# Attention queries against the keys' sums: 64-column weights in two halves of the array, in place of 128-column weights

## The chip, the cores and the metric

The kernel runs on one core of one Trainium2 chip. The metric is the device time of one execution in microseconds (us), as the median of several executions; beside it stands one execution that was recorded by the hardware profiler.

## What is computed

Three layers follow each other: linear attention, a mixture of experts with two experts per token, and a two-layer network with a squared ReLU. The change is in the first, which is computed for 4 batches, 8 heads, 576 tokens and a head dimension of 64:

```python
def phi(x):
    proj = np.einsum('bhsd,df->bhsf', x, w_phi)          # 128 features
    proj = proj - np.max(np.abs(proj), axis=-1, keepdims=True)
    return np.concatenate([np.exp(proj), np.exp(-proj)], axis=-1)   # 256 features
q_p, k_p = (phi(q), phi(k))
kv = np.einsum('bhsf,bhsd->bhfd', k_p, v)
z = np.sum(k_p, axis=2)
num = np.einsum('bhsf,bhfd->bhsd', q_p, kv)
den = np.einsum('bhsf,bhf->bhs', q_p, z)[..., None] + 1e-06
return (num / den).astype(np.float32)
```

`num` and `den` together are the queries' product with the keys' sums: for each token and head, 256 query features times a matrix that holds `kv` (64 columns), the 16 columns of the two gates already multiplied in, and `z` (1 column), 81 columns in all. That product is what the change touches.

## The kernel before

All of the attention is in fp32. Of the 576 tokens of a batch, 512 are handled as four rows of 128 tokens (`R = 4`), and the last 64 of each batch (the tail) are put together with those of the neighbouring batch.

The attention is a loop over slots `n` from 0 to 37, written out by hand as a software pipeline. A batch has nine units `u` (`i = 0` is the tails, `i = 1` to `8` the rest), and in a slot several units are at work, each at another stage. TensorE (PE) gets its instructions in this order in a slot:

- `kq_a(n)`: transposes of the next K and Q tiles (L388, L393, L399, L403) into the PSUM tile `Tk`, which ScalarE (ACT) copies to `kth` (L407).
- `k_b(n)`: K times `w_phi` into `kpair` (weights on 64 partitions, `64*128` in the profile). VectorE (DVE) takes the maximum `kmx` (L426) and subtracts it (`kd`, L428), ACT makes the two exponentials `kp` (L440, L441).
- `q_b(n - 2)`: Q times `w_phi` into `qpair`; ACT copies it to `ps` (L506), GpSimd (POOL) makes the maximum `qmx` (L508), two slots later DVE subtracts it (L513), and ACT makes the exponentials `qp` (L525, L526).
- `k_c(n - 1)`: the keys' sums into the PSUM tile `KV`, with 64-column weights (`128*64`, the values `vt` and `vtt`) and, in every second unit, 32-column weights (`128*32`, sums of the features, `zs` and `kpt` by `ones`).
- `k_d(n - 2)`, in every second unit: the keys' sums times a small matrix into `Tk` (L98 `gmat`, then `sel`), which ACT copies to `kvc` (L495). `Tk` is the one tile that the next slot's `kq_a` writes too.
- `q_d(n - 5)`: the product of the queries' features `qp` with `kvc`, into one of the PSUM tiles `N0` and `N1`, in turn. 32 such blocks are in the program. DVE divides the result by `den` with four instructions (`norm`, L532 to L544).
- In some slots then `q_tail` (the same product for the tails) and `r_3b` (the routing's ranks of tokens, from `rt_mask`).

The routing (functions `r_0` to `r_6`) runs on DVE in between, a group of four or five rows of tokens at a time, and POOL scatters finished rows to the experts' input `xg_d`. Weights of the first experts are loaded and split (L144, L145) in the same slots. After the loop, the last three units are done among the routing of the last groups, and the first expert's matmuls begin (L98 `M`).

`mm` (L98) issues one matmul; its fp32 matmuls here show as two weight loads and two streams each. The weights of `q_d` are 128 tokens' features, on 128 partitions and 128 columns (`128*128` in the profile), and `kvc`'s 81 columns are streamed past them. `q_tail` has its product in the form with 64-column weights already: two batches' tails lie in partitions 0 to 63 and 64 to 127 of the output.

Of the kernel before, what the change touches and what calls it, by code (L numbers as in the profile page):

```python
# [32 lines left out]
def kernel(  # L33
# [48 lines left out]
    def bank(tag, shape):  # L82
        if tag not in PAIRS:
            return psum.tile(shape, FT, tag=tag, name=tag)
        if pair is None:
            return pbank.tile(shape, FT, tag=tag, name=tag)
        i, half = PAIRS[tag]
        if i and mbank is not None:
            return mbank.tile(shape, FT, tag=tag, name=tag)
        names = "abc"[:len(shape) - 1]  # L90
        n = 1
        for x in shape[1:]:
            n *= x
        return pair[i][:, half, :n].rearrange(
            f"p ({' '.join(names)}) -> p {' '.join(names)}", **dict(zip(names, shape[1:])))

    def mm(o, l, r, start, stop):
        nc.tensor.matmul(o, l, r, start=start, stop=stop, skip_group_check=True)  # L98
# [157 lines left out]
    with ExitStack() as actx:  # L256
# [114 lines left out]
        KH, KP, KPT, KVB, KVZ, KVC, ZS, KE = {}, {}, {}, {}, {}, {}, {}, []  # L371
# [41 lines left out]
        def q_col(j, n):  # L413

            return j % 2 * 256 + j // 2 * n
# [114 lines left out]
        def norm(t, xo, lo):  # L530
            den = ap_.tile([128, 4], FT, name="den", tag="den", bufs=2)
            nc.vector.tensor_scalar(den, t[:, :, 80], 1e-6, None, op0=OP.add)  # L532
            yield
            rec = ap_.tile([128, 4], FT, name="rec", tag="rec", bufs=2)
            nc.vector.reciprocal(rec, den)
            yield
            if len(xo.shape) == 4:
                t = t.rearrange("p (h r) c -> p h r c", h=2)
                rec = rec.rearrange("p (h r) -> p h r", h=2)[:, :, :, None]
            else:  # L540
                rec = rec[:, :, None]
            nc.vector.tensor_mul(xo, t[..., :64], rec.to_broadcast(list(xo.shape)))
            yield
            nc.vector.tensor_mul(lo, t[..., 64:80], rec.to_broadcast(list(lo.shape)))  # L544
            yield

        def q_d(u):
            b, i = divmod(u, 9)
            if i == 0:
                return  # L550
            if i == 1:
                X[b] = ap_.tile([128, R, DM], FT, name="x", tag="x", bufs=2)
                LL[b] = ap_.tile([128, R + 1, 16, H], FT, name="ll", tag="ll", bufs=2)
            t = bank(f"N{(i - 1) % 2}", [128, R, 81])
            qp = QP.pop(u)
            half, hp = LQ[i - 1]
            for j in range(R):
                h = i - 1 if b < B - 1 else 2 * hp + j // 2
                for a in range(2):
                    mm(t[:, j], qp[:, a, q_col(j, 128):q_col(j, 128) + 128],  # L560
                       KVC[b][:, a, h // 2, (h % 2) * 81:(h % 2) * 81 + 81], j == 0 and a == 0, a == 1)
            if b < B - 1:
                ND.append(norm(t, X[b][:, :, h * 64:h * 64 + 64], LL[b][:, :R, :, h]))
            else:
                r = slice(2 * half, 2 * half + 2)
                ND.append(norm(t, X[b][:, r, hp * 128:hp * 128 + 128].rearrange("p r (h d) -> p h r d", h=2),
                               LL[b][:, r, :, 2 * hp:2 * hp + 2].rearrange("p r e h -> p h r e")))
# [253 lines left out]
        for n in range(NU + 2):  # L821
# [3 lines left out]
            b, i = divmod(n, 9)  # L825
# [43 lines left out]
            if 0 <= n - QC < NU:  # L869
                q_d(n - QC)  # L870
# [18 lines left out]
        norms(r_0(g - 1), n=1)  # L889
        q_c1(u)  # L890
        q_d(u - 2)
        r_1(g - 1)
        q_c2(u)
        q_tail(B - 1, 1, "M1")
        norms(r_2(g - 1))
        x_t(0, 0)
        x_t(0, 1)
        q_d(u - 1)
        norms(r_top(g - 1, 0))
        hold()  # L900
# [319 lines left out]
    with tc.If(most > CAP):  # L1220
        with ExitStack() as sctx:
# [27 lines left out]
            with tc.For_i(0, NT, 128) as row:  # L1249
# [8 lines left out]
                for e in range(E):  # L1258
# [4 lines left out]
                    for f in range(F // 128):  # L1263
                        t = bank(f"M{f % 2}", [128, 128])
# [3 lines left out]
                    t = bank("P", [128, DM])  # L1268
# [5 lines left out]
                for n in range(F2 // GF):  # L1274
# [4 lines left out]
                    for f in range(GF // 128):  # L1279
                        t = bank(f"M{f % 2}", [128, 128])  # L1280
# [43 lines left out]
```

## Time and profile before

| | |
|---|---|
| time, median of 3 | 1079.59 us (1079.37 to 1081.08) |
| time of the profiled execution | 1081.6 us |
| its span, first to last instruction | 1079.8 us |
| PE busy | 1057.1 us |
| DVE busy | 599.4 us |
| ACT busy | 473.9 us |
| POOL busy | 396.5 us |
| attention: end of the last `q_d` block, from the span's start | about 209.5 us |

PE is TensorE's streaming of matmuls, PEld its weight loads, which run beside the streams. Busy time of PE is modelled at the end of each matmul (an instruction's end reaches beyond the start of the next), so what a block costs is read from the start of the block to the start of the next one.

### The profile page before, as it was taken

To read this page: it belongs to the slowest core of one execution; us is meant where nothing else is said; L and a number is where in the kernel's file an instruction comes from. 1 tells how busy PE (TensorE), PEld (TensorE's weight loads), DVE (VectorE), ACT (ScalarE), POOL (GpSimd) and SP (SyncE) were. 2 spreads that over 40 slices of the span, in tenths; PEclk is the share of its full clock that TensorE was granted. 3 is DMA by queue.
4 is the path that set the end of the run, shared out by engine and by line. 5 is a ranking of instruction groups with operands and counts; after the bars stand their busy time and mean duration, and the time that the engine had idled before them with its cause. 6 is when DMAs were issued, how large, how long until landed. Compare 5 with 4: busy or idle time off the path is not lost.

```text
span 1079.8 us, 17573 instructions
## 1 busy us (share of the span) xinstructions
PE 1057.1 (98%) x6620; PEld 894.2 (83%) x6620; DVE 599.4 (56%) x1192; ACT 473.9 (44%) x967; POOL 396.5 (37%) x374
## 2 busy tenths in 40 slices
PE   7999999999999999999999999999999999999997
PEld 4777777888988888888888888888988888888885
DVE  5677788832677777686877753432443332333222
ACT  4777677424445353535354545432332222222221
POOL 3343637546645555554555464650010010000000
PEclk9999999999999999999999999999999999999999
DMA  5977524256465656565556554430120111001001
GB/s 138 269 200 220 178 80 152 98 197 207 158 198 181 210 166 205 182 204 183 187 185 198 183 164 127 126 88 1 59 69 11 39 39 40 20 0 39 1 1 41
DMA packets 104044, 136.20 MB, mean 126 GB/s; under 512 B 17554, under 2 KB 58642, under 8 KB 103954
## 3 DMA queue, kind: packets, MB, share of 16 engines
q1 hardware_dynamic: 98194, 116.14, 34.7%
q0 software_dynamic: 5760, 18.88, 5.5%
q8 instruction: 54, 0.88, 0.4%
q14 instruction: 36, 0.29, 0.1%
HBM read 92.45 MB, written 42.54 MB: 125 GB/s over the span
## 4 chain that ended last, share of the span: by engine, by line
PE 94%; DVE 3%; ACT 1%; DMA 0%; issue 0%; SPq 0%; ACTq 0%
PE M L98 38%; PE N L98 18%; PE KV L98 14%; PE Tq L98 8%; PE P L98 8%; PE kpair L98 2%; PE qpair L98 1%; PE Tk L98 1%; PE M L200 1%; PE Tk L393 1%; PE Tk L403 1%; PE Tk L1049 1%; PE Tk L200 1%; DMA kt<-in_k_dram 0%; DVE kd L428 0%; DVE kmx L426 0%
## 5 line engine op out<-in xcount | busy, mean ns | idle before, releaser
L1070 DVE TENSOR_TENSOR r<-M,r 128x512 f32<-128x512 f32 (+1 forms) x80 | 51.1, 638 | 248.3 <-ACT h2h L1069 248.3
L1066 ACT ACTIVATE r<-M 128x512 f32<-128x512 f32 (+1 forms) x80 | 44.5, 556 | 250.9 <-PE M L98 250.9
L229 ACT ACTIVATE hh<-M 128x304 fp32r<-128x304 f32 (+2 forms) x128 | 49.0, 422 | 210.7 <-PE M L98 210.7
L226 DVE SCALAR_TENSOR_TENSOR hl<-M,hh 128x304 fp32r<-128x304 f32 (+2 forms) x128 | 56.1, 470 | 109.4 <-ACT hh L229 109.3
L508 POOL PARTITION_ALL_REDUCE qmx<-ps x36 | 70.0, 1944 | 92.5 <-ACT ps L506 79.6
L1031 POOL DMA_INDIRECT ya<-y_d,yrows x18 | 18.0, 998 | 189.3 <-PE Tk L1049 113.6
L98 PE MATMUL N<-kvc,qp 128*128 128x81 f32 x512 | 63.7, 278 | 1.7 <-DVE runs L698 1.1
L98 PEld LDWEIGHTS N<-kvc,qp 128*128 128x128 f32 x512 | 59.6, 192 | 5.6 <-issue 4.6
L1071 DVE TENSOR_TENSOR h2l<-r,h2h 128x512 fp32r<-128x512 f32 (+1 forms) x80 | 57.7, 722 | 7.0
L1069 ACT ACTIVATE h2h<-r 128x512 fp32r<-128x512 f32 (+1 forms) x80 | 47.1, 589 | 2.6
L98 PE MATMUL M<-x,w30h 128*128 128x512 f32 (+1 forms) x160 | 46.1, 372 | 0.0
L98 PE MATMUL M<-x,w10h 128*128 128x512 f32 (+1 forms) x160 | 45.9, 371 | 0.0
L98 PE MATMUL M<-x,w20h 128*128 128x512 f32 (+1 forms) x160 | 45.8, 371 | 0.0
L98 PE MATMUL M<-x,w00h 128*128 128x512 f32 (+1 forms) x160 | 45.5, 369 | 0.0
L145 POOL TENSOR_TENSOR w30l<-wstage,w30h 128x512 fp32r<-128x512 f32 x20 | 27.7, 1386 | 46.3 <-ACT w30h L144 46.2
L145 POOL TENSOR_TENSOR w20l<-wstage,w20h 128x512 fp32r<-128x512 f32 x20 | 27.9, 1394 | 43.0 <-ACT w20h L144 29.4
L426 DVE TENSOR_REDUCE kmx<-kpair 128x4 f32<-128x512 f32 x36 | 24.8, 689 | 25.5 <-PE kpair L98 25.3
L767 POOL DMA_INDIRECT xg_d<-x,slots x32 | 32.4, 1014 | 12.2 <-issue 5.1
L145 POOL TENSOR_TENSOR w10l<-wstage,w10h 128x512 fp32r<-128x512 f32 x16 | 22.7, 1417 | 38.2 <-ACT w10h L144 35.2
L1001 POOL TENSOR_TENSOR wd<-wd 128x256 f32<-128x256 f32 x32 | 23.6, 737 | 35.0 <-DVE wd L997 35.0
L1001 POOL TENSOR_TENSOR wx<-wx 128x256 f32<-128x256 f32 x32 | 23.6, 738 | 34.3 <-DVE wx L997 34.0
L98 PE MATMUL KV<-kp,vt 128*64 128x256 f32 x256 | 35.6, 400 | 0.0
(432 smaller groups left out, 3271.7 us busy)
## 6 DMA issues: line engine op xcount, KB each, us to landing
wstage<-in_moe_w_dram SPq DMA_DIRECT2D x128, 256.0 KB, 3.8
xg_d<-zero SPq DMA_DIRECT2D x8, 1216.0 KB, 7.5
y_d<-y SPq DMA_DIRECT2D x32, 256.0 KB, 2.3
wide<-in_moe_w_in_dram SPq DMA_DIRECT2D x32, 256.0 KB, 3.4
wide<-in_moe_w_out_dram SPq DMA_DIRECT2D x32, 256.0 KB, 2.9
xg<-xg_d SPq DMA_DIRECT2D x7, 1024.0 KB, 6.3
kt<-in_k_dram SPq DMA_DIRECT2D x16, 256.0 KB, 4.3
vt<-in_v_dram SPq DMA_DIRECT2D x16, 256.0 KB, 4.0
```

Source lines behind the costliest of these rows:

```text
L98: nc.tensor.matmul(o, l, r, start=start, stop=stop, skip_group_check=True)
L145: (nc.gpsimd if n >= 2 else nc.vector).tensor_sub(lo[:, c], src, hi[:, c].bitcast(FT))
L226: nc.vector.scalar_tensor_tensor(hl[:, c0:c1], o, 0.0, hh[:, c0:c1].bitcast(FT), op0=OP.max, op1=OP.subtract)
L229: nc.scalar.activation(hh[:, c[1]:c[2]], c[0], AF.Relu)
L426: nc.vector.tensor_reduce(mx, t, axis=AX.X, op=OP.max, apply_absolute_value=True)
L508: nc.gpsimd.partition_all_reduce(mx, ps, 128, bass.bass_isa.ReduceOp.absmax)
L767: st = nc.gpsimd.indirect_dma_start(out=xg_d, out_offset=bass.IndirectOffsetOnAxis(ap=slots[:, T0[g] + i, c:c + 1], axis=0), in_=src, in_o ...
L1001: nc.gpsimd.tensor_mul(part, part, exp)
L1066: nc.scalar.activation(r[:, :n], t[:, :n], AF.Relu)
L1069: nc.scalar.activation(hh[:, :n], r[:, :n], AF.Square)
L1070: nc.vector.tensor_mul(r[:, :n], t[:, :n], r[:, :n])
L1071: nc.vector.tensor_sub(hl[:, :n], r[:, :n], hh[:, :n].bitcast(FT))
```

## The change

In `q_d`, each product of a row of 128 tokens is issued as two products of 64 tokens. The first has its output in partitions 0 to 63, the second in 64 to 127, and both stream the same 81 columns of `kvc`. The number of `mm` calls in a block goes from 8 to 16; the values computed are the same.

```diff
             for j in range(R):
                 h = i - 1 if b < B - 1 else 2 * hp + j // 2
                 for a in range(2):
-                    mm(t[:, j], qp[:, a, q_col(j, 128):q_col(j, 128) + 128],
-                       KVC[b][:, a, h // 2, (h % 2) * 81:(h % 2) * 81 + 81], j == 0 and a == 0, a == 1)
+                    for s in range(2):
+                        c = q_col(j, 128) + s * 64
+                        mm(t[s * 64:s * 64 + 64, j], qp[:, a, c:c + 64],
+                           KVC[b][:, a, h // 2, (h % 2) * 81:(h % 2) * 81 + 81], j == 0 and a == 0, a == 1)
```

## Rows read from the trace of the kernel before

**Rows 1.** The page's first part: busy us, share of the span, instructions.

```profile
PE 1057.1 (98%) x6620; PEld 894.2 (83%) x6620; DVE 599.4 (56%) x1192; ACT 473.9 (44%) x967; POOL 396.5 (37%) x374
```

**Rows 2.** The chain that ended last, 30 to 215 us, by line.

```profile
by line: PE N L98 27.6%; PE KV L98 22.9%; PE kpair L98 9.7%; PE qpair L98 6.7%; PE Tk L98 5.5%; PE Tk L393 3.5%; PE Tk L403 3.3%; DVE kd L428 1.9%; DVE kmx L426 1.8%; DVE ps L513 1.3%; DVE x L542 1.2%; PE M L98 1.0%; DVE rt_u L654 0.8%; ACT
```

**Rows 3.** Tile N: duration ns min/median/max, first and last start us, forms.

```profile
L98 PEld LDWEIGHTS N<-kvc,qp x512: 186/192/192, 34.4 to 209.3; 128*128 128x128 f32 x171
L98 PE MATMUL N<-kvc,qp x512: 236/275/338, 34.4 to 209.4; 128*128 128x81 f32 x171
L98 PEld LDWEIGHTS N<-kvc,qpt x64: 132/136/137, 110.3 to 118.1; 128*64 128x64 f32 x64
L98 PE MATMUL N<-kvc,qpt x64: 231/233/284, 110.3 to 118.1; 128*64 128x81 f32 x64
```

**Rows 4.** Timeline of PE, 163 to 173 us: start us, us, instructions in order.

```profile
163.77 0.62 PE L98 MATMUL KV<-zs,ones 128*32 128x128 f32 x16
164.32 2.01 PE L98 MATMUL N<-kvc,qp 128*128 128x81 f32 x16
166.17 0.38 PE L393 MATMUL Tk<-ident,kt 128*128 128x128 f32 x2
...
169.88 0.28 PE L98 MATMUL Tk<-sel,kvz 128*128 128x4 f32 x2
170.02 1.99 PE L98 MATMUL N<-kvc,qp 128*128 128x81 f32 x16
171.85 0.38 PE L393 MATMUL Tk<-ident,kt 128*128 128x128 f32 x2
172.06 0.38 PE L403 MATMUL Tk<-ident,qt 128*128 128x128 f32 x2
```

**Rows 5.** Timeline of PE, 110 to 119 us, with a block of q_tail.

```profile
115.09 2.01 PE L98 MATMUL N<-kvc,qp 128*128 128x81 f32 x16
117.03 1.34 PE L98 MATMUL N<-kvc,qpt 128*64 128x81 f32 x32
118.30 0.44 PE L393 MATMUL Tk<-ident,kt 128*128 128x128 f32 x2
118.58 0.38 PE L403 MATMUL Tk<-ident,qt 128*128 128x128 f32 x2
```

**Rows 6.** Timeline of PEld, the weight loads of that q_tail block.

```profile
117.03 1.18 PEld L98 LDWEIGHTS N<-kvc,qpt 128*64 128x64 f32 x32
```

**Rows 7.** Timeline of PE, 196 to 212 us: a change of form behind sel.

```profile
197.60 0.28 PE L98 MATMUL Tk<-sel,kvz 128*128 128x4 f32 x2
197.82 0.70 PE L98 MATMUL qpair<-kth,wf 64*128 64x256 f32 x4
```

**Rows 8.** PE's waits, 20 to 212 us: us in total, times, longest.

```profile
PE Tk L393 <- ACT kvc L495: 1.4, 4, 0.5
PE N L98 <- DVE runs L698: 1.1, 1, 1.1
PE N L98 <- DVE rt_mask L667: 1.0, 2, 0.5
```

**Rows 9.** Timeline of PE: two places where it waited, in brackets for what.

```profile
103.55 0.18 PE L98 MATMUL N<-rt_mask,before 128*128 128x32 bf16 x1 [0.47 <-DVE rt_mask L667]
...
133.64 0.44 PE L393 MATMUL Tk<-ident,kt 128*128 128x128 f32 x2 [0.29 <-ACT kvc L495]
```

**Rows 10.** Timeline of all engines, 143.5 to 145.2 us: kvc, and the next transposes.

```profile
143.31 0.44 ACT L495 ACTIVATE kvc<-Tk 128x324 f32<-128x324 f32 x1
...
144.96 0.38 PE L393 MATMUL Tk<-ident,kt 128*128 128x128 f32 x2
```

**Rows 11.** DVE's longest wait, 20 to 212 us: us in total, times, longest.

```profile
DVE kmx L426 <- PE kpair L98: 17.9, 17, 2.2
```

**Rows 12.** Busy us by stretch: PE, PEld, DVE, ACT, POOL; granted clock, DMA share, GB/s.

```profile
140.00:180.00 40.00, 39.13 (x408) 30.16 (x406) 35.37 (x99) 30.12 (x58) 23.37 (x24) 1.00 0.43 129
...
197.00:212.00 15.00, 14.49 (x174) 13.75 (x174) 13.41 (x71) 6.78 (x15) 7.52 (x13) 1.00 0.20 73
```

## The prediction

> **What bounds the kernel now.** I read the page's first part, then the chain that ended last, then the stretch in which the changed code runs. PE is busy for 98% of the span and DVE, the next, for 56% [rows 1], but that is an average over three layers, and the change touches only the attention. There the reader is to see two things. First, the chain from 30 to 215 us runs mostly along PE, and its largest share, 27.6%, is the line of the blocks that are changed [rows 2]. Of those 185 us that is 51. Second, PE hardly waits: over 20 to 212 us the three longest entries of its waits come to 3.5 us [rows 8], while DVE waits for PE's `kpair` 17 times, 17.9 us in all [rows 11]. So in this stretch PE's own stream of instructions sets the pace, and what is taken out of it is time gained, as long as the others can follow.
>
> How long a block of `q_d` holds PE is read from its start to the start of what comes next: 1.85 us from 164.32 to 166.17, behind `zs`, and 1.83 us from 170.02 to 171.85, behind `sel` [rows 4]. Sixteen weight loads with their streams take it, 0.116 us each. A load of 128 columns is recorded with 192 ns, one of 64 columns with 136 ns [rows 3]. The streams are the same 81 columns in both forms, so the larger load is what stretches the block.
>
> **What the change costs and gives.** It moves nothing to another engine and issues no DMA. It replaces 16 load-and-stream pairs in each of 32 blocks by 32 of the smaller form. That form stands in this trace: `q_tail` has the same 64-column weights on 128 partitions and the same 81 columns, two halves of the output in turn [rows 3]. A block of it has exactly 32 pairs, and takes from 117.03 to 118.30, 1.27 us [rows 5]. I take that as the price of a new block. It carries one difference that no row shows: in `q_tail` the two halves stream the `kvc` of two batches, in the new `q_d` both stream the same one. I see no reason for a price; the bound from above is the second rival.
>
> The form costs changes of mode at its ends, which the block of before did not have. Behind it, the transposes' first load is no longer issued ahead: from the K transposes to the Q transposes it takes 0.28 us behind `q_tail` [rows 5] and 0.21 behind `q_d` [rows 4]: 0.07 us more. In front of it, behind `sel`, `q_d` starts 0.14 us after `sel` did in the same form [rows 4], while a `qpair` of another form starts 0.22 after it [rows 7]. So 0.08 us is added there. Behind `zs` there was a change of form before and there is one now, so I add nothing.
>
> The Trainium skill, "TensorEngine Tiling (Array Packing)", section Tiling Modes, says that a change of tiling mode, other than a change of tile, drains TensorE; that speaks against this change. The rows above agree that it costs something, and give its size, 0.08 in front and 0.07 behind; without these the sum below would be 14.9 us and not 12.6.
>
> Now the 32 blocks by what stands around them, from the slots' order:
>
> - Nine behind `k_c`, followed by transposes of full tiles or by `k_d`: 1.85 - 1.27 - 0.07 = 0.51 each, 4.6 us. (Two of them stand behind sums with 64-column weights, where a change of mode even goes away; I leave that out.)
> - Fourteen behind `sel`: 1.83 - 1.27 - 0.07 - 0.08 = 0.41 each. Three of them are followed by a wait of PE for something that the block does not delay: twice for `rt_mask`, as at 103.55, and once for `kvc`, at 133.64 [rows 9]. There the block ends earlier and PE waits longer, and the gain is lost. Eleven remain, 4.5 us.
> - Three behind `zs` and followed by the K tails' transposes, which are in a third form. Here the block held PE as long as the one ahead of `q_tail`, which also ends in a change of form, 1.94 us [rows 5]; 1.94 - 1.27 = 0.67 each, 2.0 us.
> - Two followed by `q_tail`: now block and follower have the same form, and a change goes away at the seam, which I put at 0.1 us (the two above cost 0.07 and 0.08). 1.94 - 1.17 = 0.77 each, 1.5 us.
> - Four at the loop's end, 198 to 209.5 us. Here DVE is busy for 13.41 of 15 us [rows 12], with the last units' norms and the routing, one instruction behind the other. I count nothing for them. If PE did set the pace there, 0.6 each, 2.4 us, would be added.
>
> That is 12.6 us. What hides the rest of the work is the slack of the other engines. The nearest is `kvc`: ACT ends it at 143.75, and the transposes that write the same PSUM tile start at 144.96, 1.2 us later [rows 10]; the block between them becomes 0.4 us shorter, so 0.8 is left. Behind those transposes PE has all of the next slot queued, so a `kvc` that came later than that would cost its whole delay. DVE is the one that may fall short. From 140 to 180 us it is busy for 35.37 of 40 us [rows 12]. Six of the paying blocks lie there, 2.8 us of gain, and DVE's idle time of 4.6 us covers that only where it falls in the right slots. Around the routing groups it will not fully. I take 0.5 us off for this, one block's gain: 12.1 us.
>
> The profiled execution took 1081.6 us, with a span of 1079.8; its time would be 1069.5. The median of the runs is 1079.59, 0.2% below the profiled one; the same 12.1 us off give **1067.5 us**, and that is my forecast. What follows the attention starts 12.1 us earlier and is the same: PE stays the bound there [rows 1].
>
> **Bounds.** From above: the three lost blocks (1.2 us) and the four at the end (2.4) pay as well, the 0.5 is not lost, and the changes of mode cost half (1.1 less): 17.3 us, 1062.3. From below: DVE stops the gain wherever it is busy for over 85% of the time, in 140 to 180 us, which loses 2.8, and as much again is lost in the 50 us ahead of it, where other routing groups and the weights' splitting run on DVE: 12.1 - 2.8 - 2.8 = 6.5, 1073.1.
>
> **Rivals.**
>
> 1. *DVE becomes the pace of the attention.* For it: 88% busy in 140 to 180 us [rows 12], and waits of PE for DVE that exist already [rows 8]. Against: DVE waits for `kpair` in 17 of some 36 slots, 1.05 us in the mean [rows 11], twice what a block saves. With about half the gain lost: 6.5 us, 1073.1. It decides where DVE's work no longer fits into the shorter slot: the one from 164.32 to 170.02 [rows 4] has 5.7 us, DVE's 88% of it are 5.0, and it becomes 5.2.
>
> 2. *The two halves do not run side by side.* They stream the same `kvc` columns from the same partitions, and if PE took them one after the other, 32 streams would go at the pace of one. In `q_tail` 16 pairs of streams take some 1.12 of the 1.27 us, 0.07 a pair; alone in a row, each of the 32 would take that, 2.24 us, and with the 0.15 that are left of the 1.27 for the changes of mode 2.4: 0.55 more than before, times 28 blocks, 15 us slower, 1095. It decides where a pair takes more than about 0.1 us instead of 0.07: 1.85 less 0.15 and 0.07, over 16. Against it: the 32 loads of `q_tail`, 136 ns each, are done in 1.18 us [rows 3, 6], so loads and streams of the two halves overlap there. The Trainium skill, "TensorE: Matmul & The Clock Gate", Part 3, section The mechanism, says that loads overlap with running matmuls only when the row group differs; both halves here use all rows, so by that rule the loads would add to the streams and this rival would come out. The loads of that block disagree with it for this form [rows 6].
>
> 3. *The pairs run at twice the pace of before.* If two 64-column halves cost no more than half of two full ones, a block would be 1.85 / 2 = 0.93 us; 28 blocks save 0.92 each, 26 us, 1054. The Trainium skill's tiling page named above gives up to 2 times for a small dimension of at most 64 (section Overview). Against it, the rows of `q_tail` in the very form: 1.27 us [rows 5].
>
> 4. *The block is hidden anyway*, and PE waits as much more as it works less. It would need another engine to end last in most slots; the chain says otherwise [rows 2]. Within 2.2 us of 1079.6.
>
> **How the numbers follow.** My forecast (a gain of 8 to 17.3 us) 0.80; DVE sets the pace (2.2 to 8 us) 0.11; side by side fails (slower) 0.04; twice the pace 0.02; hidden 0.03. What a measurement of this kernel can tell from no change is about 0.2%, 2.2 us. The range reaches from the upper bound of the gain to the DVE case, 1062.3 to 1073.1, which leaves out about 2 in 10. Faster: 0.80 + 0.11 + 0.02 = 0.93; within 0.2%: 0.03; slower: 0.04.
>
> **What would show it.** In the changed kernel's profile: the blocks of `N<-kvc,qp` with 1024 loads and streams of the form `128*64`, loads of about 136 ns, and 1.27 us from a block's start to the next start; behind `sel` a start 0.2 us after it; the K transposes behind a block 0.27 us apart from the Q transposes. The last `q_d` block should end near 197.4 us. If DVE is the pace, DVE's waits for `kpair` will be nearly gone and PE's waits for `rt_mask`, `runs`, `zs` or `kvc` will have grown from 3.5 us to 7 or more. If the halves do not run side by side, the block will be 2 us or longer. I would be wrong if a block is not near 1.27 us, or if the time between 212 us and the end changes by more than 1 us.

## The result and the profile after

The changed kernel takes 1068.3 us (median of four runs, 1067.45 to 1069.16), the kernel before, beside it on the same chip, 1080.03 (1079.37 to 1081.08). The ratio is 0.9891, 95% interval 0.9873 to 0.9908: 11.7 us faster. Forecast were 1067.5, with a range of 1062.3 to 1073.1.

The profiled execution after took 1067.83 us, its span 1066.0. That is 13.8 us shorter than the profiled one of before, 2 us more than the medians say. The third layer's first matmul (`M<-x,w00h`) starts at 654.9 us after and at 667.4 before, 12.5 earlier, and 0.65 of that is start-up: the first `q_d` block starts at 33.77 instead of 34.42. In the profiles of all kernels of this study what follows that matmul took between 410.9 and 412.4 us, whichever form the blocks had. So for readings within a microsecond a milestone in the stage is the better measure, not the span of one execution. I take the stretch from the first `q_d` block to the rank matmul of the last routing group (`qpair<-rt_mask,before`, at 211.65 before and 199.17 after): 177.2 us before and 165.4 after, 11.8 shorter. Below it is "the stretch", each time of one execution.

The page's first part of the kernel after (answers to [rows 1]: 512 more matmuls and as many loads, 18 us less of PE), and the chain from 30 to 200 us by line ([rows 2]):

```profile
PE 1038.9 (97%) x7132; PEld 874.8 (82%) x7132; DVE 595.0 (56%) x1192; ACT 471.1 (44%) x967; POOL 396.7 (37%) x374
...
by line: PE KV L98 18.1%; PE N L98 12.7%; PE kpair L98 8.4%; PE qpair L98 5.5%; DVE kd L428 4.9%; PE Tk L98 4.6%; DVE kmx L426 4.5%; PE Tk L393 4.3%; DVE ps L513 3.5%; PE Tk L403 3.2%; ACT kp L440 2.2%; DVE x L542 2.2%; DVE zs L450 2.1%; AC
```

The line of the blocks was the first of the chain with 27.6% and has 12.7% now. DVE's `kmx`, `kd` and `ps` had 5.0% together [rows 2] and have 12.9%: PE still leads, and DVE is much closer behind it.

The forms of tile `N` after (duration ns min, median, max; first and last start; forms), to be read against [rows 3]:

```profile
L98 PEld LDWEIGHTS N<-kvc,qp x1024: 132/137/138, 33.8 to 195.1; 128*64 128x64 f32 x171
L98 PE MATMUL N<-kvc,qp x1024: 230/233/285, 33.8 to 195.2; 128*64 128x81 f32 x171
```

PE's timeline after, around a block behind `zs`, one behind `sel`, and one ahead of `q_tail` (answers to [rows 4, 5]):

```profile
107.85 1.34 PE L98 MATMUL N<-kvc,qp 128*64 128x81 f32 x32
109.02 1.29 PE L98 MATMUL N<-kvc,qpt 128*64 128x81 f32 x32
110.24 0.44 PE L393 MATMUL Tk<-ident,kt 128*128 128x128 f32 x2
...
154.22 0.62 PE L98 MATMUL KV<-zs,ones 128*32 128x128 f32 x16
154.77 1.34 PE L98 MATMUL N<-kvc,qp 128*64 128x81 f32 x32
156.04 0.44 PE L393 MATMUL Tk<-ident,kt 128*128 128x128 f32 x2
156.32 0.38 PE L403 MATMUL Tk<-ident,qt 128*128 128x128 f32 x2
...
159.81 0.28 PE L98 MATMUL Tk<-sel,kvz 128*128 128x4 f32 x2
160.02 1.34 PE L98 MATMUL N<-kvc,qp 128*64 128x81 f32 x32
161.29 0.44 PE L393 MATMUL Tk<-ident,kt 128*128 128x128 f32 x2
161.56 0.38 PE L403 MATMUL Tk<-ident,qt 128*128 128x128 f32 x2
```

A block takes 1.27 us (154.77 to 156.04, 160.02 to 161.29), and 1.17 ahead of `q_tail`. From `sel` to the Q transposes it was 2.18 us [rows 4] and is 1.75.

What PE waited for after, from 20 to 200 us, and DVE's wait for `kpair` (us in total, times, longest; answers to [rows 8, 11]):

```profile
PE Tk L393 <- ACT kvc L495: 4.0, 6, 1.1
PE N L98 <- DVE rt_mask L669: 1.9, 2, 1.0
PE qpair L98 <- DVE rt_mask L669: 1.3, 1, 1.3
PE N L98 <- DVE runs L700: 1.1, 1, 1.1
PE M L98 <- DVE xtl L102: 0.8, 1, 0.8
PE M L200 <- DVE ll L544: 0.7, 1, 0.7
PE N L98 <- ACT kvc L495: 0.5, 1, 0.5
...
DVE kmx L426 <- PE kpair L98: 9.8, 11, 1.7
```

PE's waits come to 10.3 us. The same list of before comes to 4.5, of which the three entries in [rows 8] are 3.5. DVE's wait for `kpair` fell from 17.9 to 9.8 us. So PE's saving went to two places, the kernel's time and longer waits of PE; DVE, with the same work in a shorter time, waits less. The windows after (columns as in [rows 12]; the loop's end is now 184 to 200), where DVE is busy for 14.55 of 16 us at the loop's end and PE for 13.23:

```profile
140.00:180.00 40.00, 38.09 (x554) 28.27 (x554) 36.05 (x102) 32.48 (x67) 27.19 (x29) 1.00 0.41 134
184.00:200.00 16.00, 13.23 (x256) 11.93 (x253) 14.55 (x75) 7.91 (x19) 8.17 (x14) 1.00 0.22 81
```

### The profile page after: what moved, and what is told of

Its sections match the earlier page's. It is cut to its first block, busy times and chain, and to the rows that moved or that the text cites. A ratio compares the mean times of both kernels' runs of the same rounds, so it can differ in the third digit from the quotient of the medians.

```text
span 1066.0 us, 18597 instructions
## 1 busy us (share of the span) xinstructions
PE 1038.9 (97%) x7132; PEld 874.8 (82%) x7132; DVE 595.0 (56%) x1192; ACT 471.1 (44%) x967; POOL 396.7 (37%) x374
## 4 chain that ended last, share of the span: by engine, by line
PE 90%; DVE 6%; ACT 2%; DMA 1%; issue 1%; POOL 0%; SPq 0%; ACTq 0%
PE M L98 38%; PE N L98 15%; PE KV L98 12%; PE Tq L98 8%; PE P L98 8%; PE kpair L98 2%; PE qpair L98 1%; DVE kd L428 1%; DVE kmx L426 1%; PE Tk L393 1%; PE M L200 1%; PE Tk L98 1%; PE Tk L1051 1%; PE Tk L200 1%; PE Tk L403 1%; DVE ps L513 1%
## 5 line engine op out<-in xcount | busy, mean ns | idle before, releaser
L1033 POOL DMA_INDIRECT ya<-y_d,yrows x18 | 17.9, 997 | 189.3 <-PE Tk L1051 113.6
L145 POOL TENSOR_TENSOR w30l<-wstage,w30h 128x512 fp32r<-128x512 f32 x20 | 27.7, 1386 | 46.7 <-ACT w30h L144 46.6
L98 PE MATMUL N<-kvc,qp 128*64 128x81 f32 x1024 | 42.6, 236 | 1.7 <-DVE runs L700 1.1
L145 POOL TENSOR_TENSOR w20l<-wstage,w20h 128x512 fp32r<-128x512 f32 x20 | 27.9, 1395 | 43.1 <-ACT w20h L144 29.4
L98 PEld LDWEIGHTS N<-kvc,qp 128*64 128x64 f32 x1024 | 37.8, 137 | 5.7 <-issue 4.4
L145 POOL TENSOR_TENSOR w10l<-wstage,w10h 128x512 fp32r<-128x512 f32 x16 | 22.9, 1434 | 38.2 <-ACT w10h L144 35.1
L1003 POOL TENSOR_TENSOR wd<-wd 128x256 f32<-128x256 f32 x32 | 23.5, 735 | 34.6 <-DVE wd L999 34.6
L1008 DVE SCALAR_TENSOR_TENSOR wd<-wd 128x256 f32<-128x256 f32 x32 | 34.1, 1067 | 1.1
```

Source lines behind the costliest of these rows:

```text
L145: (nc.gpsimd if n >= 2 else nc.vector).tensor_sub(lo[:, c], src, hi[:, c].bitcast(FT))
L1003: nc.gpsimd.tensor_mul(part, part, exp)
L1008: nc.vector.scalar_tensor_tensor(exp, ok, TINY * TINY, exp, op0=OP.is_ge, op1=OP.mult)
```

## The experiments

The theory to test had three parts: the two halves' streams run beside each other, and they and not the loads set 1.27 us; what the blocks save is time where PE leads; at the loop's end DVE leads and nothing is saved. All ratios are against the kernel before, run beside each one on the same chip.

### The halves one after the other

The same loads and streams in another order: all streams of the first half, then all of the second.

```diff
-            for j in range(R):
-                h = i - 1 if b < B - 1 else 2 * hp + j // 2
-                for a in range(2):
-                    for s in range(2):
+            for s in range(2):
+                for j in range(R):
+                    h = i - 1 if b < B - 1 else 2 * hp + j // 2
+                    for a in range(2):
```

> The same 64-column loads and streams as the changed kernel, only the order in a block differs: all 16 of the lower token half first, then all 16 of the upper half, so that neighbours in the array's order are on the same half. If the gain comes from two halves streaming side by side, a block becomes 32 streams one after the other at 0.07 us, about 2.4 us in place of 1.27, and the time is 1093 to 1099 us, slower than the kernel before (1080). If it comes from the shorter weight loads alone, the order does not matter and the time stays near 1068 us.

Measured: 1088.78 us, ratio 1.0074 (1.0059 to 1.0090). PE's timeline shows the block:

```profile
170.35 2.23 PE L98 MATMUL N<-kvc,qp 128*64 128x81 f32 x32
172.51 0.44 PE L393 MATMUL Tk<-ident,kt 128*128 128x128 f32 x2
```

2.16 us, 0.31 more than the block of before, times 28 blocks 8.7; measured 8 us slower. With nothing changed but the order, the gain becomes a loss: without the halves beside each other there is none. The smaller load has its part too. Within one half the trace has a stream start every 0.070 us; in the block of before the same 81-column streams, also one behind the other, start every 0.112 us, as far apart as their loads do, and only the weights' width differs. In the changed kernel a pair of streams, 0.006 us apart, starts every 0.070 us. So the smaller load takes a place in the row from 0.112 to 0.070 us, and the halves beside each other keep the places at 16; in order, with 32 places, the smaller load is no gain. The forecast's size was missed because I had the two halves fully apart, at 2.4 us. At the one seam in the block the second half's first streams begin while the last of the first half still run: from its first to its last start the block's 32 streams took 2.00 us, not 31 times 0.07.

### Quarters

32-column weights, four quarters in turn: twice as many loads and streams, each load smaller.

```diff
-                    for s in range(2):
-                        c = q_col(j, 128) + s * 64
-                        mm(t[s * 64:s * 64 + 64, j], qp[:, a, c:c + 64],
+                    for s in range(4):
+                        c = q_col(j, 128) + s * 32
+                        mm(t[s * 32:s * 32 + 32, j], qp[:, a, c:c + 32],
```

> 32-column weights in four token quarters, in place of 64-column ones in two halves. If the stream of the 81 columns now sets the pace of a block (0.07 us for a group that runs side by side), four quarters take as long as two halves: a block of 1.25 to 1.35 us, 1066 to 1071 us. If the weight loads still set it, the block falls to about 0.7 us and the time to 1054 to 1059. If the doubled number of instructions sets it, the block is longer and the time above 1073.

Measured: 1068.43 us, ratio 0.9889 (0.9874 to 0.9905), the changed kernel's time. The forms of `N`, and a block in PE's timeline:

```profile
L98 PEld LDWEIGHTS N<-kvc,qp x2048: 106/110/111, 33.4 to 195.2; 128*32 128x32 f32 x187
...
61.46 1.30 PE L98 MATMUL N<-kvc,qp 128*32 128x81 f32 x64
62.69 0.44 PE L393 MATMUL Tk<-ident,kt 128*128 128x128 f32 x2
```

1.23 us for 64 pairs instead of 1.27 for 32. More columns in parallel give nothing, so smaller weights are no longer what helps; 16 places in a row, at 0.07 us each, is what is left (with two halves a place is a pair of streams, with quarters four). That the larger loads made the rest of the 1.85 us before is what the halves in order show, 0.070 against 0.112 us for the same streams.

### The last four blocks in the old form

```diff
+            W = 128 if u >= 32 else 64
...
-                    for s in range(2):
-                        c = q_col(j, 128) + s * 64
-                        mm(t[s * 64:s * 64 + 64, j], qp[:, a, c:c + 64],
+                    for s in range(0, 128, W):
+                        c = q_col(j, 128) + s
+                        mm(t[s:s + W, j], qp[:, a, c:c + W],
```

> The changed kernel with the last four blocks (behind the loop's last slots) in the old 128-column form. If DVE sets the pace there, as the prediction has it, these four give nothing and the time stays at 1068.3 within 0.7 us. If PE sets the pace there, each gives 0.6 us or more and the time rises by 2.4 to 3 us, to about 1071.

Measured: 1067.84 us, ratio 0.9882 (0.9866 to 0.9897). PE's waits from 183 us to the rank matmul of the last routing group, with these four old:

```profile
PE qpair L98 <- DVE rt_mask L670: 0.5, 1, 0.5
```

In the changed kernel the same part has 2.8 us: 1.3 for `rt_mask`, 0.8 for `xtl`, 0.7 for `ll`. What the four blocks save on PE, PE then waits. The stretch is 165.4 us with these four old or new. Counting nothing for them was right.

### Only the blocks behind sel

The loop as in the experiment above, with `W` as follows: 14 blocks in the new form, 18 in the old.

```diff
+            W = 64 if u < 32 and i in (1, 3, 5, 8) else 128
```

> Only the 14 blocks behind sel in the new form, the other 18 in the old one. By the prediction's terms 11 of them gain 0.41 us and three gain nothing: 4.5 us, 1075.5. The changed kernel's trace shows two more of them followed by a wait for kvc, so 3.7 us, 1076.3. If DVE were the pace of the whole attention, the gain would be spread otherwise, and these blocks alone, with DVE far from full, would gain all of 14 times 0.41, 5.7 us, 1074.3.

Measured: 1075.58 us, ratio 0.9960 (0.9946 to 0.9973): 4.3 us of gain by the ratio (2.9 to 5.8 by its interval), where the forecast had 4.5 for these 14. The interval holds all three forecasts, 3.7, 4.5 and 5.7. The stretch is the finer measure: 172.8 us, 4.4 less than before. So the split of the sum holds in its parts: this group paid about what it should, the others, with 8.1 in the sum, the remaining 7.4.

### kvc ahead of the exponentials

After the change PE's K transposes wait 4.0 us for `kvc` in six places, five of them, 2.9 us, behind a `q_d` block. The timeline of ACT and DVE with PE behind them, at one of them:

```profile
113.56 0.68 DVE L426 TENSOR_REDUCE kmx<-kpair 128x4 f32<-128x512 f32 x1
114.27 0.69 DVE L428 TENSOR_TENSOR kd<-kpair,kmx 128x512 f32<-128x512 f32 x1
115.00 0.63 ACT L440 ACTIVATE kp<-kd 128x512 f32<-128x512 f32 x1 [2.31 <-DVE kd L428]
115.53 0.61 ACT L441 ACTIVATE kp<-kd 128x512 f32<-128x512 f32 x1
116.05 0.42 ACT L495 ACTIVATE kvc<-Tk 128x324 f32<-128x324 f32 x1
116.53 0.44 PE L393 MATMUL Tk<-ident,kt 128*128 128x128 f32 x2 [0.97 <-ACT kvc L495]
```

ACT stood idle for 2.31 us, waiting for `kd`, with `kvc` queued behind the two exponentials that need `kd`, though the matmuls that `kvc` copies (`sel`) had ended at about 114.3; then PE waited for `kvc`. The label names ACT, the late one is DVE, and the order of ACT's instructions passes its delay on. In five slots the order is turned round, so that `kvc` is copied first:

```diff
-            if n < NU:
+            late = n in (10, 19, 22, 24, 28)
+            if n < NU and not late:
                 k_e()
...
-            do(n, 4)
+            if not late:
+                do(n, 4)
             if 0 <= n - 1 < NU:
                 k_c(n - 1)
             if 0 <= n - 2 < NU - 2:
                 k_d(n - 2)
+            if late:
+                k_e()
+                do(n, 4)
```

> The changed kernel, but in five slots ACT gets its copy of kvc ahead of the two exponentials of that slot (and of the routing's small exponential). In the changed kernel's trace PE waits for kvc behind a block at 54.3, 97.8, 116.5, 126.2 and 146.7 us, 2.9 us in all. If ACT's order is what takes this part of the gain, at least three of these waits go and the time falls by 1.5 to 2.9 us, to 1065.4 to 1066.8. If DVE is the pace there and kvc only the first to show it, PE waits as long for something of DVE a little later and the time stays at 1068.3 within 0.7 us.

Measured: 1065.23 us, ratio 0.9859 (0.9844 to 0.9874): 3.1 us below the changed kernel's median, just beyond the first forecast's range, and the best version that computes everything. The stretch is 162.4 us, 3.0 shorter than in the changed kernel. PE's waits, 20 to 215 us:

```profile
PE N L98 <- DVE rt_mask L669: 1.9, 2, 1.0
PE qpair L98 <- DVE rt_mask L669: 1.3, 1, 1.3
PE N L98 <- DVE runs L700: 1.2, 1, 1.2
...
PE Tk L393 <- ACT kvc L495: 0.5, 1, 0.5
```

All five waits are gone, 2.9 us, about what the stretch gained. The 0.5 us that the K transposes still wait for `kvc` are at 26.80 us, ahead of the first `q_d` block and of all five slots (1.1 at that place in the changed kernel, 0.5 in the one before). Of the 7.1 us of waits that are left, 5.9 are for DVE.

### The same order with the old blocks

The five slots' order in the kernel before, blocks of 128 columns. The diff is the one above.

> The kernel before, with its 128-column weights, but with the five slots' order on ACT of the run with kvc first. Its trace has three of those waits, 0.9 us in all, and the longer blocks hide the other two. If the waits came up only because the blocks became shorter, this gains 0.3 to 0.9 us over the kernel before. If the order is better whatever the blocks' length, it gains 1.5 us or more.

Measured: 1078.58 us, ratio 0.9982 (0.9973 to 0.9991, 11 runs): 2.0 us (1.0 to 2.9 by its interval). The transposes' wait for `kvc` went from 1.4 [rows 8] to 0.6, 0.8 us. The profiled execution also started its first `q_d` block at 33.27 us, 1.1 earlier than the one of before; that is start-up, which differs between the profiles of this study (33.3 to 34.6), and up to slot 10 the two programs are the same. The stretch, which begins behind it, is 175.9 us, 1.3 shorter than before. So in the stretch the order is worth 1.3 us with the old blocks and 3.0 with the new. By the time, the second forecast holds; by the stretch, the gain lies between the two: the order is worth something whatever the blocks' length, and more than twice as much with the shorter blocks. The waits that it takes away, 0.8 and 2.9 us, are nearly all of the second gain; of the first 0.5 us stay open.

### The low parts of the weights on POOL

To see whether DVE holds back the rest, 12 of the 16 subtractions that make the first experts' low parts (L145) were given to POOL, on top of the change.

```diff
-        (nc.gpsimd if n >= 2 else nc.vector).tensor_sub(lo[:, c], src, hi[:, c].bitcast(FT))
+        on_pool = n >= 2 or n * 8 + i * 4 + c not in (7, 8, 11, 12)
+        (nc.gpsimd if on_pool else nc.vector).tensor_sub(lo[:, c], src, hi[:, c].bitcast(FT))
```

> The changed kernel, but 12 of the 16 subtractions that split the first experts' weights (0.69 us each) go from DVE to POOL, 8.3 us of DVE's work in the attention and at its end. If DVE is what takes the rest of the gain (its waits behind rt_mask, kd, xtl and ll), these waits shrink and the time falls to 1064 to 1066.5. If the order on ACT and PE sets them, or POOL and DVE get in each other's way, it stays at 1068.3 within 1 us or rises.

Measured: 1171.07 us, ratio 1.0854 (1.0832 to 1.0876). This tells nothing of the theory: POOL became the bound, for a reason that I had not counted. POOL's timeline (in brackets the idle time before the instruction), and DVE's longest wait, 20 to 310 us:

```profile
37.25 1.94 POOL L509 PARTITION_ALL_REDUCE qmx<-ps  x1 [2.62 <-ACT ps L507]
46.28 1.26 POOL L146 TENSOR_TENSOR w00l<-wstage,w00h 128x512 fp32r<-128x512 f32 x1 [7.09 <-ACT kth L408]
53.85 3.90 POOL L509 PARTITION_ALL_REDUCE qmx<-ps  x2 [6.31 <-issue]
...
DVE ps L514 <- POOL qmx L509: 80.7, 10, 14.9
```

### No low parts at all

The next try left the 16 subtractions out, on top of the version with `kvc` first: the low parts of the first experts' weights are set to zero by POOL, so that part of the computation is missing and 16 instructions of DVE with it.

```diff
+        if n >= 2:
+            nc.gpsimd.tensor_sub(lo[:, c], src, hi[:, c].bitcast(FT))
+        else:
+            nc.gpsimd.memset(lo[:, c].bitcast(FT), 0.0)
```

> The kernel with kvc first, but the low parts of the first experts' 16 weight pieces are left out (POOL fills them with zero), so that 16 subtractions of 0.69 us and their waits for ACT disappear from DVE in the attention. Their outputs are less exact for that. POOL gets 16 fills, which the trace before shows between its maxima without an idle stretch. If DVE sets what is left of PE's waits (for rt_mask, runs, ll and xtl, 5.9 us in the run with kvc first), they fall by a third or more and the time goes to 1061.5 to 1064. If these waits hang on the chain of the routing's own small instructions, which is as long as before, the time stays at 1065.2 within 0.8 us.

Measured: 1063.42 us, ratio 0.9839 (0.9826 to 0.9853), 1.8 us below the version that it is built on; the stretch is 160.2 us, 2.2 shorter. The four kinds of waits named in the forecast fell from 5.9 to 4.1 us, a little less than a third. PE's waits, 20 to 212 us, and DVE's wait for `kpair`:

```profile
PE N L98 <- DVE rt_mask L672: 2.0, 2, 1.0
PE qpair L98 <- DVE rt_mask L672: 1.3, 1, 1.3
PE M L98 <- DVE xtl L102: 0.8, 1, 0.8
...
DVE kmx L429 <- PE kpair L98: 20.4, 20, 1.9
```

The waits for `runs` and `ll` are gone, those for `rt_mask` are not: DVE's load sets the former; that the routing's own chain sets the latter is argued, not shown. With DVE relieved by 16 instructions only some 2 us come back. So DVE kept back only a small part, and the rival in which it sets the pace does not hold for the loop as a whole.

### The low parts a slot later

On top of the version with `kvc` first, each of the subtractions on DVE (L145) is issued one slot later, when ACT has long made the high part; in the changed kernel DVE waits for those.

```diff
+    later = {}
+
+    def w_low(n, i, c):
+        nc.vector.tensor_sub(*later.pop((n, i, c)))
...
+            at(8 + 2 * m, 1, w_low, n, i, c)
```

> The kernel with kvc first, with the 16 subtractions kept on DVE but each issued one slot later (the last one behind the routing's last group), where ACT has long made the part that it waits for. DVE waits 14.4 us in 11 places for ACT there in the changed kernel. If these waits are in front of work that PE needs, the time falls by 1 to 2.5 us, to 1062.7 to 1064.2. If DVE's wait only takes the place of its wait for kpair, nothing changes: 1065.2 within 0.8 us.

Measured: 1065.98 us, ratio 0.9862 (0.9847 to 0.9878), no gain; the stretch is 162.6 us, 0.2 longer. DVE's longest wait, 20 to 212 us:

```profile
DVE kmx L434 <- PE kpair L98: 13.2, 15, 1.9
```

DVE's waits for the high parts are gone, and its wait for `kpair` is 13.2 us instead of 8.5: it waits for PE in their place. The waits of an engine that has slack were removed without a gain. It is no clean test of them, though, since the later subtractions move other work: PE's waits for `runs`, `xtl` and `ll` fell by 1.7 us, and those for `kvc` and `kth` rose by 2.2.

### Each block in the form of what stands before it

Quarters for the blocks that follow sums with 32-column weights, halves for the others, so that no form changes in front of eleven blocks. The loop is that of the third experiment.

```diff
+            W = 32 if u < 32 and i in (2, 4, 7) else 64
```

> The changed kernel, but the 11 blocks behind zs, whose sums have 32-column weights, are in four quarters of 32 columns, so that no change of form lies ahead of them. In the run with quarters everywhere such a block starts 0.09 us after the last stream of zs in place of 0.20, and is 0.04 us shorter. If a change of form costs what the timeline shows, 11 times 0.15 is 1.6 us, less what is lost in waits: 1066.7 to 1067.6. If the doubled number of instructions costs as much, 1068.3 or more.

Measured: 1069.36 us, ratio 0.9892 (0.9876 to 0.9907): no gain in the time, a miss. In the stretch there is one, 164.7 us, 0.7 shorter than in the changed kernel: the eleven blocks start 0.11 us sooner behind `zs` and are 0.04 shorter, as expected, and PE's waits in the stretch are 0.7 us longer. A wait for `kth` is new among them (20 to 200 us):

```profile
PE Tk L98 <- ACT kth L407: 1.1, 2, 0.9
...
PE Tk L393 <- ACT kvc L495: 3.4, 6, 1.0
```

Whether that wait belongs to the shorter blocks was not tried. What hides the gain in the profiled execution lies behind the attention. From the rank matmul to the third layer's first matmul it took 457.3 us, and 455.7 both before and after. Here is the place, first in this run, then in the changed kernel (columns as in [rows 12]):

```profile
223.50:227.50 4.00, 3.96 (x15) 3.99 (x16) 0.00 (x0) 0.75 (x2) 0.00 (x0) 0.57 0.76 240
...
224.00:228.00 4.00, 4.00 (x26) 3.96 (x27) 0.53 (x1) 0.47 (x1) 0.00 (x0) 1.00 0.83 267
```

The granted clock is 0.57 in place of 1.00, most of the time at the lower of its two levels (1.2 and 2.4 GHz), and in the same 4 us PE does 15 matmuls instead of 26. Just before, PE had waited 0.4 us for a DMA and 1.2 for `xtl`; in the changed kernel it waited 1.5 us for `xtl` there and kept its clock, so why it fell stays open. The other runs of this kernel have no trace; the one with the highest mean clock, 0.999, took 1067.43 us, as long as the changed kernel's with 0.999 (1067.45). So the 0.7 us are shown in one stretch of one execution and not in the time.

## Why the prediction was right

- **The block's price.** 1.27 us was read from `q_tail`, and 1.27 us it is. The difference that no row showed, two halves that stream the same `kvc`, has no price. Here the rival in which the halves do not run side by side falls; the order of halves apart is what it would have looked like. The Trainium skill, "TensorE: Matmul & The Clock Gate", Part 3, section The mechanism, which would have loads overlap with running matmuls only where the row group differs, does not agree with these runs: 32 loads of 137 ns are 4.4 us in a block of 1.27 us, all on the same rows and beside its 32 streams.
- **Twice the pace** falls too: 1.27 and not 0.93, and quarters, with four streams in a place, go no lower than 1.23.
- **The changes of form.** Predicted 0.08 us in front, behind `sel`, and 0.07 behind. Measured 0.21 against 0.14 from `sel` to the block, 0.27 against 0.21 [rows 4] from the K to the Q transposes: 0.07 and 0.06. Ahead of `q_tail` a block takes 1.17 us, as estimated.
- **The sum.** The stretch is 11.8 us shorter, 177.23 less 165.40; the sum said 12.1. By parts, both traces laid side by side instruction by instruction: the blocks' steps are 19.2 us shorter, the steps around them, where the form changes, 2.1 longer in all, and PE's waits rose from 3.9 to 9.2, by 5.3. That is the 11.8. In the prediction's terms the blocks with their changes of form come to 16.2 (the 12.6, the 1.2 of the three lost ones and the 2.4 of the last four) where 17.1 were measured, and the losses to 4.1 where PE's waits took 5.3. That 12.1 lies so near to 11.8 is in part luck, since these two errors, 0.9 and 1.2 us, offset each other.
- **The waits.** I expected three lost blocks, 1.2 us, and 0.5 for DVE. Both groups at `rt_mask` did wait longer (1.0 to 1.9), and the `kvc` at the place of 133.64 [rows 9] too (0.87 at 126.19). Not expected were two more waits for `kvc`, 0.47 at 54.32 and 0.97 at 116.53. I had its slack at 0.8 us after the change, from one slot [rows 10]; in these slots DVE was late with `kd` and ACT's order passed that on. Waits for `kvc` in the stretch rose by 2.0 us, where the sum had 0.4 and the 0.5 for DVE. A slack read in one slot of many was too thin a ground.
- **Where DVE leads.** At 36.05 of 40 us in 140 to 180 it is at 90%, and PE's waits passed the 7 us that I gave as a sign of the rival; yet `kpair` still keeps DVE waiting, for 9.8 us, and the run without the low parts gave back some 2 us. The rival is true at the loop's end and in some slots, not for the pace. At the loop's end the forecast of 197.4 us for the end of the last `q_d` block missed: its last stream starts at 195.2. The four blocks there do end sooner, and PE's waits, 2.2 us longer, come between and behind them.
- **What follows the attention** was said to be the same. From the last rank matmul to the end it took 868.2 us before and 866.8 after, 1.4 less, which goes beyond the 1 us that I had set as a sign of being wrong. Other kernels of this study have 866.7 to 868.3 there, old blocks or new, and 869.2 where the clock fell, so it is the spread of single executions and no effect of the change: up to the third layer's first matmul it is 455.7 us in both, and all of the 1.4 lies behind that. The sign was set too tight.

## What to carry to other kernels

When an operation's weights are large beside the few columns streamed past them, look for the smaller form elsewhere in the same trace and read its price there, from the start of a block to the start of the next. Interleave the parts so that neighbours use different columns of the array; the same parts one after the other cost more than the large form. Then look at who waits next: here ACT took its instructions in the program's order and held a copy whose input was ready behind one that was waiting, and another order in five slots gave 3.0 us more, about a quarter of the main gain, of which 1.3 were to be had before the change too. Last, measure between two milestones in the stage: in one run here a granted clock that fell for 4 us in another layer cost 1.6 us, more than the gain that was looked for.

## What was not expected of the hardware

POOL stood idle at every change between PARTITION_ALL_REDUCE and TENSOR_TENSOR: 7.09 us ahead of the subtraction at 46.28, 6.31 ahead of the reduction at 53.85, and over 30 to 300 us 23 such gaps of 5.87 to 8.06 us, and the trace names no instruction that it needed: for the second none at all, for the first `kth`, which the subtraction does not read. A MEMSET in the same place, in the run without low parts, had no such gap: it starts where the reduction ends, and the next reduction waits 2.52 us for its own input.

```profile
38.42 1.94 POOL L511 PARTITION_ALL_REDUCE qmx<-ps  x1 [2.61 <-ACT ps L509]
40.24 0.60 POOL L148 MEMSET w00l<- 128x512 f32 x1
43.35 1.94 POOL L511 PARTITION_ALL_REDUCE qmx<-ps  x1 [2.52 <-ACT ps L509]
```

The Trainium skill, "GPSIMD Engine Reference", section Instruction dispatch, has about 6 us for the first call of freshly loaded code, without an instruction that shows it. The gaps here are of that size, but come at each change back and forth; that code is loaded there was not shown.
